# Reading the moving operand of TensorE's products in two interleaved strands

## The chip, the cores and the metric

One Trainium2 chip, one core of it. The metric is device microseconds of one execution of the whole kernel: median of 3 runs 882.95 us (882.77 to 883.12). The profile is that of one execution.

## The reference

```python
# 8 batches, 8 heads, 576 tokens, head size 64
kv  = einsum('bhsd,bhse->bhde', k, v)
out = einsum('bhsd,bhde->bhse', q, kv)
rms = sqrt(mean(out * out, axis=-1, keepdims=True) + 1e-06)
x   = (out / rms * g_norm)            # heads side by side: 4608 tokens x 512
h   = x @ w_in                        # 512 x 2048
P   = a[0] + a[1]*h + a[2]*h*h + a[3]*h*h*h
Q   = 1 + |b[0]|*|h| + |b[1]|*h*h
out = (P / (Q + 1e-06)) @ w_out       # 2048 x 512
```

A linear attention, normalised, and then a feed-forward layer with a rational function between its two large products.

## The kernel before

The 4608 tokens are nine tiles `t` of 512. The 2048 hidden columns are sixteen chunks `c` of 128. A pair (t, c) is a **slot**, and the loop at line 808 walks the 144 slots in order. Everything is issued by hand in the order of the code (line 709), so each engine works through its own queue in that order, and the engines wait for one another by semaphores alone.

In slot i the loop issues, for TensorE, first `gemm2` of the slot two back (L537: chunk c's 128 columns of g times four token blocks, into the four accumulators `acc`), then whatever part of the attention of the next tile stands at this c (tables `attention0` and `attention2`, L439 to L451), and then `gemm1` of the next slot (L468: 128 columns of h for 512 tokens, into `ph`). ScalarE, VectorE and GpSimd work on the slot's own h: `ew_a`, `ew_b`, `ew_c` and `ew_d` (L489 to L532) evaluate the rational function. Their first instruction in a slot is ScalarE's L494, which reads `ph`; their last are L530 (high part of g, ScalarE) and L531 (low part of g, GpSimd), issued a slot later.

**Precision.** From chunk 4 of tile 0 on for `gemm1`, and from chunk 12 of tile 0 on for `gemm2`, each operand is split into a high and a low float32r part, and a product is three TensorE instructions: high times high, low times high, high times low. `gemm1` of a slot is then 4 x 3 = 12 instructions of L486, `gemm2` 4 x 3 = 12 of L551 (L596 at the very end): 24 in a slot, each with its own weight load of 128 columns and 512 moving columns. Before those chunks a product is one plain float32 instruction (L479 and L544), while the split weights are still being made.

**What moves and what stays.** In `gemm1` the stationary operand is a 128 x 128 block of w_in, and the moving one is x (`x[t][kc]`, or `xf` where it is plain): 128 partitions by 512 tokens. In `gemm2` the stationary operand is a 128 x 128 block of g, and the moving one is w_out's chunk: 128 partitions by 512 columns. So far both are read in the order in which they lie.

**The attention** of tile t+1 runs in the slots of tile t. `att_o` (L373) multiplies the kv matrices with q, which lies as 128 partitions by 512 tokens, in two runs of columns where a tile takes tokens of two batches (64 t of the earlier batch, the rest of the later one); from tile 2 on each run is three instructions (L385 to L387), in tile 1 one (L381). Its result, its squares, the sums of squares (L406), the normalised `xf` and its split into x keep the order in which q's tokens lie. At chunk 9 the kv products of a later batch and the sums of squares stand (L344, L406). At chunk 14 ScalarE casts the next tile's x (L249).

**The end of a tile.** At chunk 1 of the next tile, after the last `gemm2` of a tile, `evacuate` (L553) has ScalarE and VectorE copy the four accumulators out (L560, L558); the next `gemm2`, chunk 0 of the new tile, writes the same four banks.

**Tile 0** also converts the weights from 64-bit words and splits them, by the table `first_tiles` (L153).

On the host, `kernel()` (L853) lays q out as `qT` (L868) and w_out in chunks (L878).

Of the kernel before, what the change touches and what calls it, by code (L numbers as in the profile page):

```python
# [23 lines left out]
def linear_attention_then_rational_ffn(  # L24
# [10 lines left out]
    PE, ACT, DVE, POOL = nc.tensor, nc.scalar, nc.vector, nc.gpsimd  # L35

    NB, NPAIR = kv.shape[:2]
    NT, DM = out.shape
    NF = w_in.shape[0]
    P = 128  # L40
    D = 64
    S = NT // NB
    TW = 512
# [28 lines left out]
    kvf = wpool.tile([P, 2, NPAIR, P], F32, tag="f7", name="kvf")  # L72
# [47 lines left out]
    def unsplit1(t, c):  # L120
        return t == 0 and c < 4
# [67 lines left out]
    raws, ups, w32, whl, wparts = {}, {}, {}, {}, {}  # L189
# [129 lines left out]
    xs, x = {}, {}  # L319
    kvq, qs, sqs, rs, rbs, xf = {}, {}, {}, {}, {}, {}  # L320
# [3 lines left out]
    def fetch_kv(t, p):  # L324
        kvms[t, p] = m = work.tile([P, 2, 5, P], F32, tag="kvm", name=f"kvm_{t}_{p}", bufs=NPAIR)
        nc.sync.dma_start(m, kv[t, p])
# [40 lines left out]
    def att_kvp(t, p):  # L367
        if t + 1 < NB:
            kv_products(t + 1, p, kvps[t + 1][:, p])
            if t + 2 < NB:  # L370
                fetch_kv(t + 2, p)

    def att_o(t, p):  # L373
        ps = ps_at.tile([P, TW], F32, tag="at", name=f"op_{t}_{p}", bufs=1)
        q = qs.pop((t, p))
        n0 = D * t
        for bt, cs in ((t - 1, slice(0, n0)), (t, slice(n0, TW))):
            if cs.start == cs.stop:
                continue
            if t == 1:  # L380
                PE.matmul(ps[:, cs], kvf[:, bt, p], q[:, cs], start=True, stop=True)  # L381
                continue
            qh, ql = q
            kh, kl = kvh[bt % 2][:, p], kvl[bt % 2][:, p]
            PE.matmul(ps[:, cs], kh, qh[:, cs], start=True, stop=False)  # L385
            PE.matmul(ps[:, cs], kl, qh[:, cs], start=False, stop=False)  # L386
            PE.matmul(ps[:, cs], kh, ql[:, cs], start=False, stop=True)  # L387
        sq = work.tile([P, TW], F32, tag="at", name=f"sq_{t}_{p}", bufs=4)
        xf[t, p] = xpool.tile([P, TW], F32, tag=f"xf{p}", name=f"xf_{t}_{p}")
        ACT.activation(sq, ps, AF.Square)  # L390
        ACT.activation(xf[t, p], ps, AF.Copy, scale=ghalf)
        sqs[t, p] = sq
        if t == 1:
            next_q(t, p)
# [62 lines left out]
    acc = {}  # L457
# [6 lines left out]
    def in_turn(behind, n):  # L464
        each = [(k, j) for k in range(n) for j in range(3) if j != behind]
        return each if behind is None else each + [(k, behind) for k in range(n)]

    def gemm1(t, c):  # L468
        if t == NTILE - 1 and c % 3 == 2:
            ph = ps_at.tile([P, TW], F32, tag="at", name=f"h_{t}_{c}", bufs=1)  # L470
        else:
            ph = ps_h.tile([P, TW], F32, tag="h", name=f"h_{t}_{c}")
        gemm1_part(t, c, ph, slice(0, TW))
        return ph

    def gemm1_part(t, c, ph, cs, kcs=range(NPAIR)):
        if unsplit1(t, c):
            for kc in kcs:
                PE.matmul(ph, w32["wi", c][:, kc * P:(kc + 1) * P], xf[t, kc], start=(kc == 0), stop=(kc == NPAIR - 1))  # L479
            return  # L480
        order = in_turn(behind1.get((t, c)), NPAIR)
        for n, (kc, j) in enumerate(order):
            xh, xl = (f[:, cs] for f in x[t][kc])
            wh, wl = (f[:, kc * P:(kc + 1) * P] for f in whl["wi", c])
            w, f = ((wh, xh), (wl, xh), (wh, xl))[j]
            PE.matmul(ph, w, f, start=(n == 0), stop=(n == len(order) - 1))  # L486
# [50 lines left out]
    def gemm2(t, c):  # L537
        g = gs.pop((t, c))
        first, last = c == 0, c == NF - 1
        if first:  # L540
            acc[t] = [ps_acc.tile([P, DM], F32, tag="acc", name=f"acc_{t}_{s}") for s in range(NSUB)]
        if unsplit2(t, c):
            for s in range(NSUB):
                PE.matmul(acc[t][s], g[:, s * P:(s + 1) * P], w32["wo", c], start=first, stop=last)  # L544
            return
        (gh, gl), (wh, wl) = g, whl["wo", c]
        products = (gh, wh), (gh, wl), (gl, wh)
        order = in_turn(behind2.get((t, c)), NSUB)
        for n, (s, j) in enumerate(order):
            a, w = products[j]  # L550
            PE.matmul(acc[t][s], a[:, s * P:(s + 1) * P], w, start=first and j == 0, stop=last and all(k != s for k, _ in order[n + 1:]))  # L551

    def evacuate(t):  # L553
        for k in range(NSUB // 2):
# [9 lines left out]
    def finish(t, ph):  # L564
        c = NF - 1
        parts = [slice(k * TW // 2, (k + 1) * TW // 2) for k in range(2)]
        rooms = ("d", 2), ("q", 2), ("u", 2), ("gh", 2), ("gl", 2)
        spare = ("qr", 1), ("qh", 1), ("ql", 1), ("rb", 2), ("rb", 2)
        halves = []
        for n, tags in enumerate((rooms, spare)):  # L570
            new = [work.tile([P, TW // 2], F32 if m < 3 else F32R, tag=tag, name=f"{'vquab'[m]}_last_{n}", bufs=bufs) for m, (tag, bufs) in enumerate(tags)]
            halves.append((*new, ps_at.tile([P, TW // 2], F32, tag=("r", "at")[n], name=f"r_last_{n}", bufs=1)))
        for k, (v, q, u, gh, gl, r) in zip(parts, halves):
            ACT.activation(v, ph[:, k], AF.Abs, scale=b1)
            ACT.activation(u, ph[:, k], AF.Identity, bias=na[:, 2:3], scale=na[:, 3:4])
        ew_d(t, c - 1)
        for k, (v, q, u, gh, gl, r) in zip(parts, halves):
            DVE.scalar_tensor_tensor(q, v, b0abs, ph[:, k], ALU.add, ALU.mult)
            DVE.tensor_tensor(u, u, ph[:, k], ALU.mult)
            DVE.scalar_tensor_tensor(u, u, na[:, 1:2], ph[:, k], ALU.add, ALU.mult)  # L580
            ACT.activation(q, q, AF.Abs)
            ACT.activation(r, q, AF.Ln, bias=bias[:, 2:3], scale=QSC)
            ACT.activation(r, r, AF.Exp, bias=bias[:, 3:4], scale=-1.0)
        gemm2(t, c - 2)
        for v, q, u, gh, gl, r in halves:
            DVE.scalar_tensor_tensor(u, u, na[:, 0:1], r, ALU.add, ALU.mult)
            DVE.scalar_tensor_tensor(r, q, QEPS, r, ALU.add, ALU.mult)
            DVE.scalar_tensor_tensor(u, r, 2.0, u, ALU.subtract, ALU.mult)
            ACT.copy(gh, u)
            DVE.tensor_tensor(gl, u, f32(gh), ALU.subtract)  # L590

        def products(c, gs, order, s0=0):
            wh, wl = whl["wo", c]
            for s, j in order:
                a, w = ((gs[0], wh), (gs[0], wl), (gs[1], wh))[j]
                PE.matmul(acc[t][s], a[:, (s - s0) * P:(s - s0 + 1) * P], w, start=False, stop=c == NF - 1 and j == 2)  # L596

        def store(s, by):
            ob = work.tile([P, DM], F32, tag="at", name=f"ob_{t}_{s}", bufs=4)
            r0 = t * TW + s * P  # L600
            if by is not None:
                copy(by, ob, acc[t][s])
                nc.sync.dma_start(out[r0:r0 + P], ob)
                return
            for e, (by, queue) in enumerate(((DVE, nc.sync), (ACT, ACT))):
                es = slice(e * DM // 2, (e + 1) * DM // 2)
                copy(by, ob[:, es], acc[t][s][:, es])
                queue.dma_start(out[r0:r0 + P, es], ob[:, es])

        before = gs[t, c - 1]  # L610
        products(c - 1, before, [(s, j) for s in range(2) for j in range(3)])
        products(c, halves[0][3:5], [(s, j) for s in range(2) for j in range(2)] + [(s, 2) for s in range(2)])
        store(0, DVE)
        store(1, ACT)
        for s, by in (2, DVE), (3, None):
            products(c - 1, before, [(s, j) for j in range(3)])
            products(c, halves[1][3:5], [(s, j) for j in range(3)], 2)
            store(s, by)
# [140 lines left out]
    conv_b2(("wi", 2), one)  # L759
    scale_low(("wi", 2), ACT, two)  # L760
    h00 = ps_h.tile([P, TW], F32, tag="h", name="h_0_0")
    gemm1_part(0, 0, h00, slice(0, TW), (0,))
    first_rb(1)
    first_warm(3, 1)
    first_rb(3)
# [3 lines left out]
    scale_low(("wo", 0), ACT, both)  # L769
    first_norm(3)  # L770
    scale_high(("wi", 2), DVE, two)
    gemm1_part(0, 0, h00, slice(0, TW), (1,))
    conv_b2(("wi", 0), two)
    first_rb(2)
    first_norm(2)
    gemm1_part(0, 0, h00, slice(0, TW), (2,))
    gemm1_part(0, 0, h00, slice(0, TW), (3,))
    fetch_kv(1, 0)
    fetch_q(1, 0)
    for u in fetch_at[-1]:  # L780
# [4 lines left out]
    ph = h00  # L785
# [22 lines left out]
    for i, (t, c) in enumerate(slots[:-1]):  # L808
# [12 lines left out]
        if i < 4:  # L821
            ph = gemm1(0, i + 1)
        if t + 1 < NTILE:
# [4 lines left out]
            if i == MOVE[0]:  # L828
                last = work.tile([P, 2 * DM], F32, tag="rb", name="w_last", bufs=2)
# [6 lines left out]
        if t == NTILE - 1:  # L836
            ahead += [gemm1(*slots[k]) for k in ((i + 1, i + 2) if c == 0 else (i + 2,)) if k < len(slots)]
            ph = ahead.pop(0) if ahead else None
        elif i >= 4:
            ph = gemm1(*slots[i + 1])  # L840
        if c == NF - 2 and 0 < t < NTILE - 1:
            xl = [split(t + 1, p) for p in range(NPAIR)]
# [48 lines left out]
```

## Time and profile before

| | |
|---|---|
| median of 3 runs | 882.95 us |
| span of the profiled execution | 881.1 us |
| TensorE busy (matmul) | 873.4 us, 99% |
| TensorE weight loads | 694.1 us, 79% |
| VectorE / ScalarE / GpSimd busy | 684.2 / 696.7 / 330.5 us |
| DMA | 65.93 MB, mean 75 GB/s |

The page gives a matmul's duration from its start to its modelled end, which lies in the next one or two; so the busy share of TensorE says little, and the time that a product takes is read as the distance from one start to the next. Engine names: PE is TensorE, PEld its weight load, ACT ScalarE, DVE VectorE, POOL GpSimd.

### The profile page before, as it was taken

Reading aid. Unit: us, or ns where it says so; the run is one execution under the profiler, and the core shown is the slowest. Engines: PE = TensorE matmul, PEld = TensorE weight load, DVE = VectorE, ACT = ScalarE, POOL = GpSimd, SP = SyncE. Lnnn points to the kernel's source line nnn. Section 1 sums busy time; section 2 is a strip of 40 time slices with the busy share of each in tenths; the row PEclk is TensorE's granted clock in tenths of the full one; section 3 lists DMA queues with packets and bytes.
Section 4 is the critical chain, followed back from the end, with each engine's and each line's share of the span. In section 5 each row is a group of like instructions: output and inputs, shape, how many; then the busy total and the mean of one; then the engine's idle time right before and its main releaser. Section 6 shows DMA issues by size and latency. Waiting matters only on the chain.

```text
span 881.1 us, 11990 instructions
## 1 busy us (share of the span) xinstructions
PE 873.4 (99%) x4370; PEld 694.1 (79%) x4370; DVE 684.2 (78%) x1022; ACT 696.7 (79%) x1129; POOL 330.5 (38%) x265
## 2 busy tenths in 40 slices
PE   8999999999999999999999999999999999999998
PEld 5466578888888888888888888888888878788886
DVE  3999998968876788668866886588767877787876
ACT  5999889878886778867886888678877788778775
POOL 3586672525242333224332423242433333332221
PEclk9999999999999999999999999999999999999999
DMA  9683541131111302050103211020102010101001
GB/s 361 261 322 132 146 154 73 36 132 49 48 36 61 120 1 72 25 166 3 60 24 133 49 48 36 14 49 21 52 25 49 1 63 22 49 1 48 1 1 48
DMA packets 24191, 65.93 MB, mean 75 GB/s; under 512 B 2372, under 2 KB 2756, under 8 KB 24132
## 3 DMA queue, kind: packets, MB, share of 16 engines
q1 hardware_dynamic: 23968, 65.04, 21.9%
q8 instruction: 34, 0.56, 0.3%
q14 instruction: 25, 0.20, 0.1%
q10 hardware_dynamic: 164, 0.14, 0.0%
HBM read 55.59 MB, written 9.57 MB: 74 GB/s over the span
## 4 chain that ended last, share of the span: by engine, by line
PE 96%; DVE 2%; ACT 1%; issue 0%; POOL 0%; ACTq 0%; DVEq 0%; POOLq 0%
PE h L486 43%; PE acc L551 39%; PE acc L544 5%; PE ms L344 2%; PE h L479 1%; PE ms L406 1%; PE op L386 1%; PE op L387 1%; PE op L385 1%; PE kvp L653 1%; PE acc L596 1%; PE op L381 0%; PE op L662 0%; PE idle L644 0%; PE rb L701 0%; DVE q L497 0%
## 5 line engine op out<-in xcount | busy, mean ns | idle before, releaser
L486 PE MATMUL h<-x,wiparts 128*128 128x512 f32 x1680 | 409.8, 393 | 0.0
L486 PEld LDWEIGHTS h<-x,wiparts 128*128 128x128 f32 x1680 | 313.4, 188 | 70.4 <-issue 4.6
L531 POOL TENSOR_TENSOR gl<-u,gh 128x512 fp32r<-128x512 f32 x131 | 172.1, 1314 | 431.6 <-ACT gh L530 355.3
L513 DVE SCALAR_TENSOR_TENSOR u<-u,na,r 128x512 f32<-128x512 f32 x143 | 106.6, 745 | 85.5 <-ACT r L507 85.3
L497 DVE SCALAR_TENSOR_TENSOR q<-v,b0abs,h 128x512 f32<-128x512 f32 x143 | 106.2, 743 | 72.3 <-ACT u L495 71.3
L494 ACT ACTIVATE v<-h,b 128x512 f32<-128x512 f32 x143 | 98.6, 690 | 79.0 <-PE h L486 78.6
L551 PE MATMUL acc<-woparts,gh 128*128 128x512 f32 x400 | 124.8, 391 | 0.4 <-ACT ob L560 0.4
L551 PE MATMUL acc<-woh,gh 128*128 128x512 f32 x320 | 124.7, 390 | 0.0
L551 PE MATMUL acc<-woh,gl 128*128 128x512 f32 x320 | 124.6, 390 | 0.0
L503 ACT ACTIVATE q<-q 128x512 f32<-128x512 f32 x143 | 90.5, 633 | 40.7 <-DVE q L497 39.4
L551 PE MATMUL acc<-wol,gh 128*128 128x512 f32 x320 | 122.2, 390 | 0.0
L495 ACT ACTIVATE u<-h,na 128x512 f32<-128x512 f32 x143 | 111.0, 776 | 0.0
L504 DVE SCALAR_TENSOR_TENSOR u<-u,na,h 128x512 f32<-128x512 f32 x143 | 106.9, 748 | 5.1
L530 ACT CAST gh<-u 128x512 fp32r<-128x512 f32 x131 | 81.3, 620 | 34.9 <-DVE u L520 24.7
L506 ACT ACTIVATE r<-q,bias 128x512 f32<-128x512 f32 x143 | 99.0, 692 | 4.5
L514 DVE SCALAR_TENSOR_TENSOR r<-q,r 128x512 f32<-128x512 f32 x143 | 98.4, 688 | 0.0
L507 ACT ACTIVATE r<-r,bias 128x512 f32<-128x512 f32 x143 | 94.7, 662 | 4.7
L498 DVE TENSOR_TENSOR u<-u,h 128x512 f32<-128x512 f32 x143 | 97.3, 680 | 0.0
L520 DVE SCALAR_TENSOR_TENSOR u<-r,u 128x512 f32<-128x512 f32 x131 | 90.5, 691 | 4.2
L551 PEld LDWEIGHTS acc<-woparts,gh 128*128 128x128 f32 x400 | 74.6, 188 | 17.8 <-ACT r L507 1.6
L551 PE MATMUL acc<-woparts,gl 128*128 128x512 f32 x200 | 78.0, 390 | 0.0
L551 PEld LDWEIGHTS acc<-woh,gh 128*128 128x128 f32 x320 | 60.1, 188 | 12.4
(139 smaller groups left out, 869.6 us busy)
## 6 DMA issues: line engine op xcount, KB each, us to landing
kvm<-in_kv_dram SPq DMA_DIRECT2D x28, 640.0 KB
raw_wo<-in_w_out_dram SPq DMA_DIRECT2D x8, 1024.0 KB
qr<-in_qT_dram SPq DMA_DIRECT2D x32, 256.0 KB
rb<-rd SPq DMA_DIRECT2D x32, 256.0 KB
out_dram<-ob SPq DMA_DIRECT2D x16, 512.0 KB
raw_wi<-in_w_in_dram SPq DMA_DIRECT2D x6, 1024.0 KB
first<-in_first_dram SPq DMA_DIRECT2D x4, 640.0 KB
raw_wi<-in_w_in_dram SPq DMA_DIRECT2D x4, 512.0 KB
```

Of the source, the lines that this page charges most:

```text
L486: PE.matmul(ph, w, f, start=(n == 0), stop=(n == len(order) - 1))
L494: ACT.activation(v, ph, AF.Abs, scale=b1)
L495: ACT.activation(u, ph, AF.Identity, bias=na[:, 2:3], scale=na[:, 3:4])
L497: DVE.scalar_tensor_tensor(q, v, b0abs, ph, ALU.add, ALU.mult)
L498: DVE.tensor_tensor(u, u, ph, ALU.mult)
L504: DVE.scalar_tensor_tensor(u, u, na[:, 1:2], ph, ALU.add, ALU.mult)
L506: ACT.activation(r, q, AF.Ln, bias=bias[:, 2:3], scale=QSC)
L507: ACT.activation(r, r, AF.Exp, bias=bias[:, 3:4], scale=-1.0)
L513: DVE.scalar_tensor_tensor(u, u, na[:, 0:1], r, ALU.add, ALU.mult)
L514: DVE.scalar_tensor_tensor(r, q, QEPS, r, ALU.add, ALU.mult)
L531: POOL.tensor_tensor(gl, u, f32(gh), ALU.subtract)
L551: PE.matmul(acc[t][s], a[:, s * P:(s + 1) * P], w, start=first and j == 0, stop=last and all(k != s for k, _ in order[n + 1:]))
```

## The change

Both large stages read their moving operand through `strands`: the 512 columns are taken as two halves, and the order is column 0 of the first half, column 0 of the second, column 1 of the first, and so on. Two consecutive columns lie 256 columns (1024 bytes) apart. So that results come out in their true order, the host lays q's tokens and w_out's columns out in the inverse order: of each 512, the even ones first and then the odd ones. All that comes between q and x keeps that order. `att_o` has a tile's tokens of two batches in two runs in each half, and reads and writes each run as two blocks, one in each half; the number of columns per instruction is the same. The number of instructions, their sizes, the DMA transfers and the work of the other engines stay as they are.

```diff
+    def halves(f):
+        return f.rearrange("p (a b) -> p a b", a=2)
+
     def att_o(t, p):
...
-        n0 = D * t
-        for bt, cs in ((t - 1, slice(0, n0)), (t, slice(n0, TW))):
+        n0 = D * t // 2
+        for bt, cs in ((t - 1, slice(0, n0)), (t, slice(n0, TW // 2))):
             if cs.start == cs.stop:
                 continue
+            to = halves(ps)[:, :, cs]
             if t == 1:
-                PE.matmul(ps[:, cs], kvf[:, bt, p], q[:, cs], start=True, stop=True)
+                PE.matmul(to, kvf[:, bt, p], halves(q)[:, :, cs], start=True, stop=True)
                 continue
-            qh, ql = q
+            qh, ql = (halves(f)[:, :, cs] for f in q)
             kh, kl = kvh[bt % 2][:, p], kvl[bt % 2][:, p]
-            PE.matmul(ps[:, cs], kh, qh[:, cs], start=True, stop=False)
+            PE.matmul(to, kh, qh, start=True, stop=False)
...
+    def strands(f):
+        return f.rearrange("p (a b) -> p b a", a=2)
+
...
-                PE.matmul(ph, w32["wi", c][:, kc * P:(kc + 1) * P], xf[t, kc], start=(kc == 0), stop=(kc == NPAIR - 1))
+                PE.matmul(ph, w32["wi", c][:, kc * P:(kc + 1) * P], strands(xf[t, kc]), start=(kc == 0), stop=(kc == NPAIR - 1))
...
-            xh, xl = (f[:, cs] for f in x[t][kc])
+            xh, xl = (strands(f) for f in x[t][kc])
...
-                PE.matmul(acc[t][s], g[:, s * P:(s + 1) * P], w32["wo", c], start=first, stop=last)
+                PE.matmul(acc[t][s], g[:, s * P:(s + 1) * P], strands(w32["wo", c]), start=first, stop=last)
...
-            PE.matmul(acc[t][s], a[:, s * P:(s + 1) * P], w, start=first and j == 0, stop=last and all(k != s for k, _ in order[n + 1:]))
+            PE.matmul(acc[t][s], a[:, s * P:(s + 1) * P], strands(w), start=first and j == 0, stop=last and all(k != s for k, _ in order[n + 1:]))
...
-    qT = q.reshape(B, H // 2, 2, S, D).transpose(1, 2, 4, 0, 3).reshape(H // 2, 2 * D, B * S)
+    qT = q.reshape(B, H // 2, 2, S, D).transpose(1, 2, 4, 0, 3).reshape(H // 2, 2 * D, B * S // 512, 256, 2)
+    qT = qT.swapaxes(3, 4).reshape(H // 2, 2 * D, B * S)
...
-        "w_out": w_out.view(_np.int64).reshape(DF // 128, 128, DM),
+        "w_out": w_out.view(_np.int64).reshape(DF // 128, 128, DM // 2, 2).swapaxes(2, 3).reshape(DF // 128, 128, DM),
```

The line of the last products (L596) takes `strands(w)` in the same way.

## Rows read from the trace of the kernel before

**Rows 1.** The page: busy shares, and the granted clock in 40 slices.

```profile
PE 873.4 (99%) x4370; PEld 694.1 (79%) x4370; DVE 684.2 (78%) x1022; ACT 696.7 (79%) x1129; POOL 330.5 (38%) x265
...
PEclk9999999999999999999999999999999999999999
```

**Rows 2.** The page: the chain that ended last, by engine and by line.

```profile
PE 96%; DVE 2%; ACT 1%; issue 0%; POOL 0%; ACTq 0%; DVEq 0%; POOLq 0%
```

**Rows 3.** Timeline of PE, tile 3: start us, us, engine, line, operation, count.

```profile
357.40 2.88 PE L486 MATMUL h<-x,wiparts 128*128 128x512 f32 x12
360.12 0.39 PE L551 MATMUL acc<-woh,gh 128*128 128x512 f32 x1
```

**Rows 4.** Timeline of PE, tile 3: the attention's products with 256 moving columns.

```profile
351.33 0.28 PE L386 MATMUL op<-qh,kvl 128*128 128x256 f32 x1
...
351.93 0.63 PE L486 MATMUL h<-x,wiparts 128*128 128x512 f32 x2
```

**Rows 5.** Plain float32 products: timeline of PE in tile 0, and their group's mean.

```profile
71.14 3.59 PE L544 MATMUL acc<-wow,g 128*128 128x512 f32 x8
L544 PE MATMUL acc<-wow,g 128*128 128x512 f32 x96 | 43.3, 594 | 0.0
```

**Rows 6.** Timeline of PE, tile 6: the 12 products right behind an att_o.

```profile
647.04 3.02 PE L486 MATMUL h<-x,wiparts 128*128 128x512 f32 x12
649.89 0.39 PE L551 MATMUL acc<-woh,gh 128*128 128x512 f32 x1
```

**Rows 7.** Busy time by stretch: tile 0, tile 1 to chunk 8, tile 3's chunks 2 to 13.

```profile
26.40:132.50 106.10, 105.57 (x496) 64.44 (x495) 103.17 (x137) 95.44 (x151) 75.29 (x44) 1.00 0.55 195
132.50:184.60 52.10, 52.10 (x239) 43.42 (x238) 47.50 (x72) 46.86 (x78) 20.71 (x16) 1.00 0.15 50
331.30:403.60 72.30, 72.30 (x410) 60.08 (x410) 52.34 (x79) 55.82 (x92) 25.30 (x20) 1.00 0.25 81
```

**Rows 8.** ACT's waits for h: tile 1 to chunk 8, tile 1 from there, tile 3's chunks 2 to 13.

```profile
ACT v L494 <- PE h L486: 0.5, 1, 0.5
ACT v L494 <- PE h L486: 7.8, 5, 5.0
L494 ACT ACTIVATE v<-h,b 128x512 f32<-128x512 f32 x12 | 8.3, 690 | 10.5 <-PE h L486 10.5
```

**Rows 9.** Timeline around a tile's end: ACT at chunk 14 and at the copies out.

```profile
403.62 0.69 ACT L494 ACTIVATE v<-h,b 128x512 f32<-128x512 f32 x1 [1.21 <-PE h L486]
...
410.15 0.68 ACT L494 ACTIVATE v<-h,b 128x512 f32<-128x512 f32 x1
...
415.42 0.68 ACT L494 ACTIVATE v<-h,b 128x512 f32<-128x512 f32 x1
...
420.28 0.68 ACT L494 ACTIVATE v<-h,b 128x512 f32<-128x512 f32 x1
...
425.14 1.07 ACT L560 COPY ob<-acc 128x512 f32<-128x512 f32 x2
```

**Rows 10.** Timeline of PE at the same place in tile 3: the first gemm2 of a tile.

```profile
330.57 0.84 PE L486 MATMUL h<-x,wiparts 128*128 128x512 f32 x3
331.34 0.47 PE L551 MATMUL acc<-woparts,gh 128*128 128x512 f32 x1
```

**Rows 11.** Timeline of ACT in tile 7: three slots with attention in them.

```profile
718.39 0.69 ACT L494 ACTIVATE v<-h,b 128x512 f32<-128x512 f32 x1 [0.30 <-PE h L486]
724.51 0.69 ACT L494 ACTIVATE v<-h,b 128x512 f32<-128x512 f32 x1 [0.30 <-PE h L486]
730.63 0.69 ACT L494 ACTIVATE v<-h,b 128x512 f32<-128x512 f32 x1 [0.30 <-PE h L486]
```

**Rows 12.** Groups of instructions by line: the products of att_o.

```profile
L385 PE MATMUL op<-qh,kvh 128*128 128x128 f32 (+7 forms) x52 | 15.2, 293 | 0.0
L381 PE MATMUL op<-qr,kvf 128*128 128x64 f32 (+1 forms) x16 | 4.6, 408 | 0.0
```

**Rows 13.** Timeline at tile 4's start: a low part of g, and its first reader.

```profile
418.40 1.30 POOL L531 TENSOR_TENSOR gl<-u,gh 128x512 fp32r<-128x512 f32 x1 [4.49 <-ACT gh L530]
...
420.19 0.39 PE L551 MATMUL acc<-woparts,gl 128*128 128x512 f32 x1
```

More of the change, by code (lines that the diff above doesn't have):

```diff
@@ L375, in att_o @@
         q = qs.pop((t, p))
-        n0 = D * t
-        for bt, cs in ((t - 1, slice(0, n0)), (t, slice(n0, TW))):
+        n0 = D * t // 2
+        for bt, cs in ((t - 1, slice(0, n0)), (t, slice(n0, TW // 2))):
             if cs.start == cs.stop:
                 continue
+            to = halves(ps)[:, :, cs]
             if t == 1:
-                PE.matmul(ps[:, cs], kvf[:, bt, p], q[:, cs], start=True, stop=True)
+                PE.matmul(to, kvf[:, bt, p], halves(q)[:, :, cs], start=True, stop=True)
                 continue
-            qh, ql = q
+            qh, ql = (halves(f)[:, :, cs] for f in q)
             kh, kl = kvh[bt % 2][:, p], kvl[bt % 2][:, p]
-            PE.matmul(ps[:, cs], kh, qh[:, cs], start=True, stop=False)
-            PE.matmul(ps[:, cs], kl, qh[:, cs], start=False, stop=False)
-            PE.matmul(ps[:, cs], kh, ql[:, cs], start=False, stop=True)
+            PE.matmul(to, kh, qh, start=True, stop=False)
+            PE.matmul(to, kl, qh, start=False, stop=False)
+            PE.matmul(to, kh, ql, start=False, stop=True)
         sq = work.tile([P, TW], F32, tag="at", name=f"sq_{t}_{p}", bufs=4)
@@ L472, in gemm1, with gemm1_part @@
             ph = ps_h.tile([P, TW], F32, tag="h", name=f"h_{t}_{c}")
-        gemm1_part(t, c, ph, slice(0, TW))
+        gemm1_part(t, c, ph)
         return ph
-    def gemm1_part(t, c, ph, cs, kcs=range(NPAIR)):
+    def gemm1_part(t, c, ph, kcs=range(NPAIR)):
         if unsplit1(t, c):
             for kc in kcs:
-                PE.matmul(ph, w32["wi", c][:, kc * P:(kc + 1) * P], xf[t, kc], start=(kc == 0), stop=(kc == NPAIR - 1))
+                PE.matmul(ph, w32["wi", c][:, kc * P:(kc + 1) * P], strands(xf[t, kc]), start=(kc == 0), stop=(kc == NPAIR - 1))
             return
@@ L595, in products @@
                 a, w = ((gs[0], wh), (gs[0], wl), (gs[1], wh))[j]
-                PE.matmul(acc[t][s], a[:, (s - s0) * P:(s - s0 + 1) * P], w, start=False, stop=c == NF - 1 and j == 2)
+                PE.matmul(acc[t][s], a[:, (s - s0) * P:(s - s0 + 1) * P], strands(w), start=False, stop=c == NF - 1 and j == 2)
         def store(s, by):
@@ L761, in linear_attention_then_rational_ffn @@
     h00 = ps_h.tile([P, TW], F32, tag="h", name="h_0_0")
-    gemm1_part(0, 0, h00, slice(0, TW), (0,))
+    gemm1_part(0, 0, h00, (0,))
     first_rb(1)
@@ L771, in linear_attention_then_rational_ffn @@
     scale_high(("wi", 2), DVE, two)
-    gemm1_part(0, 0, h00, slice(0, TW), (1,))
+    gemm1_part(0, 0, h00, (1,))
     conv_b2(("wi", 0), two)
@@ L775, in linear_attention_then_rational_ffn @@
     first_norm(2)
-    gemm1_part(0, 0, h00, slice(0, TW), (2,))
-    gemm1_part(0, 0, h00, slice(0, TW), (3,))
+    gemm1_part(0, 0, h00, (2,))
+    gemm1_part(0, 0, h00, (3,))
     fetch_kv(1, 0)
```

## The prediction

> **What bounds the kernel now.** I read the busy shares and the clock first. TensorE counts as busy 99% of the span and its granted clock is full, 2.4 GHz, in all 40 slices [rows 1]; the chain that ended last lies 96% on it [rows 2]. A matmul's end is modelled, so neither says that a product takes the time that it must. For that I go to the timeline and take distances between starts. In a steady stretch twelve products begin at 357.40 and the next thing at 360.12 [rows 3]: 2.72 us / 12 = 226.7 ns a product. At 2.4 GHz 512 columns are 213.3 ns, so 13.3 ns, 32 cycles, go into something else, and this happens 3264 times: 140 of the 144 slots have a split gemm1 and 132 a split gemm2, 12 each.
>
> Is this excess per column or per product? The attention's products with half as many columns answer it: five starts from 351.33 to 351.93 [rows 4] are 120 ns each, and 256 columns are 106.7, so again 13.3. It is per product, and each product has one weight load of 128 columns beside it. The plain float32 products show something else: eight take 3.59 us [rows 5], less the last one's 0.594 that is 3.00 / 7 = 428 ns from start to start, 2 x 214: two passes, with an excess of about 1 ns each, though a weight load runs beside them too. So the excess belongs to products that consume one fresh 4-byte column per cycle, and goes where each column is held for two. A third reading: right behind an att_o, with the weight loads at another phase to the products, the same twelve take 2.85 us [rows 6], 237.5 ns each. Twelve products of one kind with the same neighbours differ by 5% with that phase alone. My reading is that weight loads and the moving operand get in each other's way at the memory, about 32 cycles a product when steady.
>
> **Where a shorter product would show.** By stretch [rows 7]: in tile 0 VectorE is busy 103.17 of 106.10 us, so the conversions set the pace and TensorE's time there is worth nothing. In tile 1 up to chunk 8 ScalarE waits for h only once, 0.5 us [rows 8]: the elementwise chain is level with TensorE, and a faster product gains nothing. From there on ScalarE waits for h in nearly every slot: 7.8 us in the rest of tile 1, 10.5 us in the twelve slots of tile 3 from chunk 2 to 13 [rows 8]. Those are bound by TensorE. Around the end of each tile it is the other way: from chunk 14's h, for which ScalarE waited 1.21 us, the next three slots start with no wait at all, and the chain runs on to the copies of the accumulators at 425.14, 21.5 us later [rows 9]. The new tile's first gemm2 waits for these copies already now: its first start comes where three steady products would end it, 330.57 + 3 x 0.227 = 331.25, and is seen at 331.34, and it lasts 0.47 us in place of 0.39 [rows 10]: 0.17 us in all. TensorE's four slots there can get faster and will only wait longer.
>
> **The change part by part.** *Removed and added:* no instruction. *The moving order* is the one term that counts. No row shows a product that reads two strands, so I bound it. Best case by the nearest row: the excess goes as in the plain float32 products, 428 / 2 = 214 ns, a gain of 12.7 ns (226.7 - 214). Worst case by the nearest row: 237.5 ns, a loss of 10.8, if the weight loads collide as in the stretch behind att_o. Far worst: every column costs as much as in a plain float32 product, 428 ns, a loss of 201. I take the best case. Two strands 1024 bytes apart mean that each place in memory is visited every second cycle, which is what the float32 products do by holding each column for two, and those lose nothing to the same loads.
>
> [...]
>
> *Sum.* Tiles 2 to 8: twelve slots of 24 products, from the first gemm2 behind the copies to the h that starts the next boundary (in tile 8, to the last h, behind which the closing elementwise chain is fixed): 288 x 12.7 ns = 3.66 us, times 7 = 25.6 us. Tile 1: the five slots in which ScalarE waits, 120 x 12.7 ns = 1.5 us. Tile 0, the start, tile 1 to chunk 8 and the boundaries: nothing. Total 27.1 us, for 2136 products.
>
> *Is there cover for it?* A slot gets 24 x 12.7 = 305 ns shorter. ScalarE's tightest waits are 0.30 us in tile 7's attention slots [rows 11]: just enough, to within their rounding. At the boundary four slots of TensorE shrink by 1.2 us in all, which becomes a wait for the copies. Before that, a low part of g is finished at 419.70 and first read at 420.19 [rows 13], 0.49 us to spare, less than the 0.9 us by which TensorE comes earlier there; this stall only takes part of the later one's place.
>
> *att_o's blocks:* 156 instructions of L385 to L387 (three lines of 52) and 16 of L381 [rows 12] read and write two blocks in place of one. At zero, as the columns are as many; above, if each block cost like a product of its own with its 13.3 ns, 172 x 13.3 = 2.3 us, exposed; below zero nothing, since no weight load is saved. *Plain float32 products* (L479, L544) are 128 and lie in tile 0 and ahead of it; they take two cycles a column already, so zero, and at most a doubling to 856 ns, 55 us, part of it beside VectorE. *Host layout:* same bytes and run lengths in every transfer, zero.
>
> The profile's span is 881.1 us; the median of the runs, 882.95, is 1.85 above it, which I leave as it is. 882.95 - 27.1 = 855.9, so **856 us**, 3.1% less.
>
> **The rivals.** *No change.* If the 32 cycles are the array's own turn from one set of weights to the next, at the rate of one column a cycle, the order of the columns is indifferent, and the time is 883. For it: the excess is the same at 256 and 512 columns. Against: the 237.5 ns behind att_o, which a fixed cost would not give. [...]
>
> *Slower.* [...] It decides as soon as a product takes over 227 ns, because TensorE has no slack in tiles 1 to 8: 3072 products there. At 237.5 ns that is 3072 x 10.8 = +33 us, 916 us; at 428 ns 3072 x 201 = +617 us, about 1500 us, plus what tile 0 can't hide. For it: in this kernel's rows every operand of a product is read in order, so nothing shows that another order is free. [...]
>
> **How the numbers follow.** The gain 0.60, no change 0.15, slower 0.25 (half of it around 916, half far above). The forecast's own range is 848 to 870: down to 848 if boundaries and tile 1 shrink too (3072 x 12.7 = 39 us is the ceiling, 844), up to 870 if half of the 13.3 ns goes. The range over the cases is 848 to 918: it takes in no change and the near end of slower, and leaves out the far end and a little of the gain's tails, about 0.18. A difference under 0.2% can't be told from none by a measurement of this kernel; faster by more than that 0.60, within 0.15, slower 0.25.
>
> **What would show it.** Right: twelve products of L486 in a steady slot from start to start take about 2.57 us in place of 2.72; ScalarE's waits for h in chunks 2 to 13 fall from 10.5 us a tile to 7; TensorE's gap at the first gemm2 of a tile grows from 0.17 to over 1 us; tile 0 keeps its 106 us. Wrong: the 2.72 us stay (no change), or rise (slower); if they fall and tile times don't, an elementwise chain that I took to have room has none.

## The result and the profile after

The changed kernel takes **867.94 us** (867.73 to 868.07, 4 runs) against 882.89 us of the kernel before on the same chip: a ratio of 0.9829, with an interval of 0.9815 to 0.9843. It is 15 us faster, where 27 were forecast. The span of the profiled execution goes from 881.1 to 866.3 us. Two effects of opposite sign make up this difference of 14.8 us, and both can be read from the trace.

The page of the changed kernel, busy shares and the chain that ended last (against [rows 1, 2]):

```profile
PE 853.2 (98%) x4370; PEld 696.0 (80%) x4370; DVE 687.7 (79%) x1022; ACT 699.3 (81%) x1129; POOL 328.1 (38%) x265
...
PE 61%; DVE 19%; ACT 17%; issue 2%; DMA 1%; SPq 0%; ACTq 0%; DVEq 0%
```

The chain lay 96% on TensorE and now lies 61% on it: the elementwise engines end more of the waits. Line numbers have moved: L486 is now L493, L551 is L558, L479 and L544 are L486 and L551, L494 is L501.

The timeline of TensorE in the changed kernel (start us, us, engine, line, operation, count): plain products in tile 0, the first gemm2 of tile 3, a steady gemm1 with the attention's products ahead of it, and a gemm1 behind an att_o in tile 6:

```profile
36.21 4.58 PE L551 MATMUL acc<-wow,g 128*128 128x512 f32 x8
...
330.71 0.48 PE L558 MATMUL acc<-woparts,gl 128*128 128x512 f32 x1 [0.33 <-POOL gl L538]
...
332.97 2.75 PE L493 MATMUL h<-x,wiparts 128*128 128x512 f32 x12
336.22 0.67 PE L558 MATMUL acc<-woparts,gh 128*128 128x512 f32 x2 [0.50 <-ACT r L514]
...
355.26 0.28 PE L390 MATMUL op<-qh,kvl 128*128 128x256 f32 x1
...
355.85 2.75 PE L493 MATMUL h<-x,wiparts 128*128 128x512 f32 x12
358.44 0.38 PE L558 MATMUL acc<-woh,gh 128*128 128x512 f32 x1
...
641.00 2.84 PE L493 MATMUL h<-x,wiparts 128*128 128x512 f32 x12
643.68 0.38 PE L558 MATMUL acc<-woh,gh 128*128 128x512 f32 x1
```

Read the distances. Twelve split products take from 355.85 to 358.44: 2.59 us, **215.8 ns each**, where they took 226.7 [rows 3]. Behind an att_o they take 2.68 us where they took 2.85 [rows 6]. There the first of the twelve stands apart, as the shortest, middle and longest modelled lengths show (ns; the kernel before, then the changed one). Each such length is 163 ns more than the distance to the next start, to within 2 ns:

```profile
L486 PE MATMUL h<-x,wiparts x12: 387/395/477, 647.0 to 649.7; 128*128 128x512 f32 x12
L493 PE MATMUL h<-x,wiparts x12: 379/379/462, 641.0 to 643.5; 128*128 128x512 f32 x12
```

The first product takes 314 ns in order and 299 in strands. The other eleven take 224 to 236 ns in order, but 215 or 216 throughout in strands.

The plain float32 products went the other way. The first eight of tile 0, in the kernel before, and the whole group's mean in the changed one:

```profile
34.62 3.70 PE L544 MATMUL acc<-wow,g 128*128 128x512 f32 x8
...
L551 PE MATMUL acc<-wow,g 128*128 128x512 f32 x96 | 54.0, 705 | 0.0
```

The same eight take 4.58 us instead of 3.70, and the mean length is 705 ns instead of 594 [rows 5]. From start to start, the first of the eight left out, it is **540 ns instead of 428**. The attention's products of 256 columns, which now read and write two blocks, still follow one another at 118 ns (355.26 to 355.85, five starts; 120 in [rows 4]).

Busy time by stretch in the changed kernel (length; then PE, PEld, DVE, ACT and POOL busy; clock, DMA share, GB/s): tile 0, tile 1 to chunk 8, the boundary of tiles 2 and 3, tile 3's chunks 2 to 13. The last line is ScalarE's wait for the h of a split gemm1 in tile 0 (us in all, times, longest):

```profile
27.00:142.40 115.40, 115.40 (x493) 64.26 (x492) 107.92 (x137) 97.94 (x149) 75.00 (x44) 1.00 0.49 176
142.40:193.80 51.40, 51.26 (x245) 44.63 (x244) 46.84 (x72) 46.48 (x76) 20.52 (x16) 1.00 0.16 54
329.00:337.00 8.00, 7.17 (x33) 5.67 (x32) 7.16 (x12) 6.93 (x12) 2.57 (x2) 1.00 0.00 0
336.20:405.20 69.00, 68.98 (x409) 60.38 (x410) 51.32 (x78) 55.91 (x91) 24.10 (x19) 1.00 0.26 85
...
ACT v L501 <- PE h L493: 6.5, 5, 2.3
```

Tile 1's first chunk starts at 142.4 us instead of 132.5: **9.9 us lost up to there**. From there to the end the kernel needs 723.9 us instead of 748.6: **24.7 us won**. Tile 3's twelve slots shrink from 72.3 to 69.0 us [rows 7]. In tile 0 of the kernel before, no wait of ScalarE for h is longer than 0.1 us.

ScalarE in the changed kernel: its group L501 in tile 3's chunks 2 to 13 (busy, mean ns, idle before and who ended it), and its timeline over the end of tile 3:

```profile
L501 ACT ACTIVATE v<-h,b 128x512 f32<-128x512 f32 x12 | 8.3, 688 | 6.8 <-PE h L493 6.5
```

```profile
405.22 0.69 ACT L501 ACTIVATE v<-h,b 128x512 f32<-128x512 f32 x1 [0.38 <-PE h L493]
...
426.97 1.07 ACT L567 COPY ob<-acc 128x512 f32<-128x512 f32 x2
```

The wait for h fell from 10.5 us [rows 8] to 6.5. From chunk 14's h to the copies it is 21.75 us, as it was (21.5 in [rows 9]): this stretch belongs to the elementwise chain. TensorE now waits there, 0.33 us for a low part of g at 330.71, and then again at 336.22: the block that began at 332.97 needs 2.59 us, up to 335.56, so 0.66 us pass before the first gemm2 of the new tile.

### The profile page after: what moved, and what is told of

Same layout as the page of the kernel before. It is cut to its first block, busy times and chain, and to the rows that moved or that the text cites. A ratio compares the mean times of both kernels' runs of the same rounds, so it can differ in the third digit from the quotient of the medians.

```text
span 866.3 us, 11993 instructions
## 1 busy us (share of the span) xinstructions
PE 853.2 (98%) x4370; PEld 696.0 (80%) x4370; DVE 687.7 (79%) x1022; ACT 699.3 (81%) x1129; POOL 328.1 (38%) x265
## 4 chain that ended last, share of the span: by engine, by line
PE 61%; DVE 19%; ACT 17%; issue 2%; DMA 1%; SPq 0%; ACTq 0%; DVEq 0%
PE h L493 24%; PE acc L558 21%; PE acc L551 6%; ACT r L513 5%; ACT r L514 4%; DVE u L520 4%; ACT q L510 4%; DVE q L504 4%; DVE r L521 4%; DVE u L527 4%; PE h L486 2%; DVE x L316 2%; PE ms L344 2%; PE ms L410 1%; PE op L391 1%
## 5 line engine op out<-in xcount | busy, mean ns | idle before, releaser
L493 PE MATMUL h<-x,wiparts 128*128 128x512 f32 x1680 | 390.2, 382 | 0.0
L493 PEld LDWEIGHTS h<-x,wiparts 128*128 128x128 f32 x1680 | 315.2, 189 | 50.4 <-issue 4.1
L501 ACT ACTIVATE v<-h,b 128x512 f32<-128x512 f32 x143 | 98.3, 688 | 55.8 <-PE h L493 53.4
L558 PE MATMUL acc<-woparts,gh 128*128 128x512 f32 x400 | 120.3, 380 | 3.5 <-ACT r L514 2.5
L558 PE MATMUL acc<-woh,gh 128*128 128x512 f32 x320 | 121.3, 379 | 0.0
L558 PE MATMUL acc<-woh,gl 128*128 128x512 f32 x320 | 121.3, 379 | 0.0
L558 PE MATMUL acc<-wol,gh 128*128 128x512 f32 x320 | 118.9, 379 | 0.4 <-POOL wol L269 0.4
L558 PEld LDWEIGHTS acc<-woparts,gh 128*128 128x128 f32 x400 | 75.1, 189 | 16.2 <-ACT r L514 4.3
L558 PE MATMUL acc<-woparts,gl 128*128 128x512 f32 x200 | 76.9, 384 | 1.7 <-POOL gl L538 1.5
L558 PEld LDWEIGHTS acc<-wol,gh 128*128 128x128 f32 x320 | 60.5, 189 | 9.3 <-POOL wol L269 0.8
```

The source lines that it names most:

```text
L558: PE.matmul(acc[t][s], a[:, s * P:(s + 1) * P], strands(w), start=first and j == 0, stop=last and all(k != s for k, _ in order[n + 1:]))
```

## The experiments

Eleven kernels were run. Two questions stood behind them: is the loss of 9.9 us in tile 0 the plain products' own, and why does a split product gain 10.9 ns?

### The two kinds of products apart

`a_split_only`: strands for the split products; the plain ones, and with them all w_out products of tile 0, in order. Tile 0's order is put right where g is written and where its accumulators are copied out.

```diff
-                PE.matmul(ph, w32["wi", c][:, kc * P:(kc + 1) * P], strands(xf[t, kc]), ...)
+                PE.matmul(ph, w32["wi", c][:, kc * P:(kc + 1) * P], xf[t, kc], ...)
...
-                PE.matmul(acc[t][s], g[:, s * P:(s + 1) * P], strands(w32["wo", c]), ...)
+                PE.matmul(acc[t][s], g[:, s * P:(s + 1) * P], w32["wo", c], ...)
...
-            PE.matmul(acc[t][s], a[:, s * P:(s + 1) * P], strands(w), ...)
+            PE.matmul(acc[t][s], a[:, s * P:(s + 1) * P], strands(w) if t else w, ...)
...
+        if unsplit1(t, c):
+            g, r, u = g.rearrange("p (b a) -> p a b", a=2), halves(r), halves(u)
         DVE.scalar_tensor_tensor(g, r, 2.0, u, ALU.subtract, ALU.mult)
...
+                if t == 0:
+                    ACT.copy(ob[:, s].rearrange("p (b a) -> p a b", a=2), halves(acc[t][2 * k + s]))
```

> Strands for the split products only; the plain float32 products of tile 0, and all of tile 0's w_out products, read in order again (the order is put right where g of chunks 0 to 3 is written and where tile 0's accumulators are copied out). Theory one, the plain products pay for the strands: they go from 540 ns back to 428 ns from start to start, 128 x 112 ns = 14 us of TensorE, tile 1 begins near 132.5 us in place of 142.4, and the time is about 858 us. Theory two, tile 0 is late for another reason (the blocks of att_o, or another phase of its waits): tile 1 still begins later than 138 us and the time stays over 864.

Measured: **861.30 us** (861.06 to 861.49, 5 runs), 0.9756 of the kernel before (0.9743 to 0.9769), so faster than both kernels. Its tile 0 by stretch, and two groups by line (busy us, mean ns, idle before; the second one of tile 0 alone, and under it the same group in the kernel before):

```profile
26.30:135.30 109.00, 104.84 (x496) 64.23 (x495) 106.00 (x137) 97.77 (x150) 75.32 (x44) 1.00 0.53 192
```

```profile
L553 PE MATMUL acc<-wow,g 128*128 128x512 f32 x96 | 43.5, 595 | 0.7 <-POOL wow L242 0.7
...
L237 DVE SCALAR_TENSOR_TENSOR wiw<-raw_wi,wiw 128x1024 int32<-128x1024 int32 x6 | 9.8, 1635 | 0.0
...
L237 DVE SCALAR_TENSOR_TENSOR wiw<-raw_wi,wiw 128x1024 int32<-128x1024 int32 x6 | 8.6, 1432 | 0.0
```

The plain products are back (mean 595 ns as in [rows 5], 705 in the changed kernel), and tile 1 starts at 135.3: 7.1 of the 9.9 us return, and the time is 3.3 us over the 858 of theory one. From there to the end it takes 724.2 us, against 723.9 in the changed kernel: the 24.7 us won are kept. Theory two asked for over 138 and over 864, and falls. What is left, 2.8 us, lies where VectorE sets the pace: the same 137 instructions are busy 106.00 us instead of 103.17 [rows 7]. The six of L237 for w_in, for one, take 1635 ns each where they took 1432. All its conversions in tile 0 (L211, L232, L237, L242, L269) take 43.4 us instead of 40.2. They are longer in the changed kernel and in `b_plain_only` too (45.4 and 43.4 us), which don't put tile 0's order right, so that edit doesn't explain it. Why the conversions got longer stays open.

`b_plain_only` is the opposite: strands in the plain products alone.

```diff
-            xh, xl = (strands(f) for f in x[t][kc])
+            xh, xl = x[t][kc]
...
-            PE.matmul(acc[t][s], a[:, s * P:(s + 1) * P], strands(w), ...)
+            PE.matmul(acc[t][s], a[:, s * P:(s + 1) * P], w, ...)
```

> Strands for the plain float32 products of tile 0 only; all split products read in order (tokens and columns come out in mixed order). Theory one, the plain products' loss is their own: 540 ns, tile 1 begins near 142 us, split products 226.7 ns, and the time is about 893 us, 10 over the kernel before. Theory two, tile 0's loss comes from elsewhere: tile 1 begins near 133 us and the time is about 883.

Measured: 895.28 us in one run. Tile 0 of it by stretch, ScalarE's wait for h there, and TensorE's timeline:

```profile
27.00:144.80 117.80, 117.80 (x493) 64.03 (x492) 107.21 (x138) 95.91 (x149) 73.72 (x44) 1.00 0.48 172
...
ACT v L501 <- PE h L493: 11.9, 8, 2.6
```

```profile
36.19 4.58 PE L551 MATMUL acc<-wow,g 128*128 128x512 f32 x8
...
358.45 2.91 PE L493 MATMUL h<-x,wiparts 128*128 128x512 f32 x12
361.20 0.39 PE L558 MATMUL acc<-woh,gh 128*128 128x512 f32 x1
```

The plain products have the 4.58 us of the changed kernel, and tile 1 starts at 144.8, 12.3 us late. Theory one holds, from both sides. ScalarE's wait shows how: it waits 11.9 us for h in tile 0, where it had no such wait in the kernel before, so TensorE has become the slower one there. Of the 2.4 us over the changed kernel's 142.4, some 1.7 go with tile 0's 156 split products of gemm1, which are in order here (an estimate: 156 x 10.9 ns). From tile 1 to the end it takes 748.7 us, as the kernel before does (748.6). It has the host's layout and att_o's blocks of the changed kernel, so neither of these costs anything that shows.

### Which order helps

Five kernels read all products in other orders. Only the line in `strands` changes:

```diff
-        return f.rearrange("p (a b) -> p b a", a=2)
+        return f.rearrange("p (c a b) -> p c b a", a=2, b=4)   # p_near
+        return f.rearrange("p (a b) -> p b a", a=4)            # p_quarters
+        return f.rearrange("p (b a) -> p a b", a=2)            # p_evenodd
+        return f.rearrange("p (a b k) -> p b a k", a=2, k=2)   # p_pairs
+        return f.rearrange("p (a b k) -> p b a k", a=2, k=4)   # p_lines
```

What was expected:

> All products read in strands that lie only 16 bytes apart: columns 0, 4, 1, 5, 2, 6, 3, 7 and so on (tokens and columns come out in another order). Theory one, any order in which columns that follow one another are no neighbours: 216 ns for split products. Theory two, the places must be far apart: 227 ns or more. Plain products: 540 ns if leaving the neighbour is what costs them.

> All products read four strands of 128 columns, 512 bytes apart, in place of two of 256 (tokens and columns come out in another order). Theory one, any order in which two columns that follow one another are no neighbours in memory frees the split products: 216 ns again. Theory two, the two places must be exactly two, or 1024 bytes apart: over 220 ns, up to 227 or more. Plain products: if they pay for every column that leaves its neighbour, 540 ns again; if they pay per strand, more.

> All products read the even columns and then the odd ones, a step of 8 bytes (tokens and columns come out in another order). Theory one, any order in which columns that follow one another are no neighbours: 216 ns for split products. [...] Plain products: 428 ns if one walk suffices, 540 if leaving the neighbour is what costs.

> All products read two strands 1024 bytes apart, but two neighbouring columns of each at a time (tokens and columns come out in another order). Theory one, changing the place at each column is what frees the split products: between 216 and 227 ns. Theory two, two places in alternation are enough at any grain: 216 ns. Plain products: half of the loss, about 484 ns, if each change of place costs; 540 if the second place costs.

> All products read two strands 1024 bytes apart, four neighbouring columns of each at a time (tokens and columns come out in another order). Theory one, changing the place at each column is what frees the split products: 227 ns, as in order. Theory two, two places in alternation are enough at any grain: 216 ns. Plain products: about 456 ns if each change of place costs the same, 428 if a group of four columns is as good as a walk in order.

Measured, in this order: 868.12, 1107.79, 1617.57, 1230.37 and 956.20 us, one run each. Timelines of TensorE, one fence for each kernel in the same order: eight plain products, then a split gemm1 and what follows it.

```profile
36.19 4.61 PE L551 MATMUL acc<-wow,g 128*128 128x512 f32 x8
...
397.44 2.75 PE L493 MATMUL h<-x,wiparts 128*128 128x512 f32 x12
400.03 0.38 PE L558 MATMUL acc<-woh,gh 128*128 128x512 f32 x1
```

```profile
44.01 7.23 PE L551 MATMUL acc<-wow,g 128*128 128x512 f32 x8
...
400.53 3.45 PE L493 MATMUL h<-x,wiparts 128*128 128x512 f32 x12
403.81 0.44 PE L558 MATMUL acc<-woh,gh 128*128 128x512 f32 x1
```

```profile
34.93 3.87 PE L551 MATMUL acc<-wow,g 128*128 128x512 f32 x8
...
404.30 5.65 PE L493 MATMUL h<-x,wiparts 128*128 128x512 f32 x12
409.77 0.64 PE L558 MATMUL acc<-woh,gh 128*128 128x512 f32 x1
```

```profile
34.89 3.89 PE L551 MATMUL acc<-wow,g 128*128 128x512 f32 x8
...
402.66 4.17 PE L493 MATMUL h<-x,wiparts 128*128 128x512 f32 x12
406.66 0.83 PE L558 MATMUL acc<-woparts,gh 128*128 128x512 f32 x2
```

```profile
34.38 3.70 PE L551 MATMUL acc<-wow,g 128*128 128x512 f32 x8
...
395.78 3.17 PE L493 MATMUL h<-x,wiparts 128*128 128x512 f32 x12
398.79 0.41 PE L558 MATMUL acc<-woh,gh 128*128 128x512 f32 x1
```

The distance from the first start of a gemm1 to what follows, by twelve, beside the median distance between the starts of two plain products of gemm2 in that kernel's trace. The eight plain products shown include a longer first one each; in the kernel before, the first such eight take 3.70 us.

| order of the 512 columns | split, ns each | plain, ns each |
|---|---|---|
| as they lie | 226.7 | 429 |
| two strands, 1024 bytes apart | 215.8 | 540 |
| two strands, 16 bytes apart | 215.8 | 543 |
| two strands, four columns of each at a time | 251 | 429 |
| two strands, two columns of each at a time | 333 | 453 |
| four strands, 512 bytes apart | 273 | 873 |
| even columns, then odd ones | 456 | 451 |

The medians over all split products of gemm1 agree with the second column to within about 1%, except for four strands, where the median is 283 ns.

No theory of the pair covers this. "Any order in which neighbours don't follow one another" is refuted by the even columns, 456 ns, and by four strands, 273 ns. "The two places must lie far apart" is refuted by the strands 16 bytes apart, which do as well as those 1024 apart, 215.8 ns both. And two places in alternation are not enough either: with two or four columns at a time they lose, at 333 and 251 ns against 226.7. Of the orders tried, what helps is narrow: two strands, one column at a time.

The plain products rank the orders otherwise. As they lie, or with four columns of each strand at a time, one takes 429 ns. With two at a time, or in even columns, it takes 451 to 453. By single columns it takes 540 and 543 in two strands, 26% more, and 873 in four. Why is not shown by any run.

### What the excess in order belongs to

`w_half` loads half as many stationary columns for a third of the gemm1 products of the kernel before, from tile 1 on, and leaves the other half of these products out; `w_half_strands` does the same to the changed one.

```diff
-            PE.matmul(ph, w, f, start=(n == 0), stop=(n == len(order) - 1))
+            half = slice(0, P // 2 if t and j == 1 else P)
+            PE.matmul(ph[half], w[:, half], f, start=(n == 0), stop=(n == len(order) - 1))
```

> The kernel before, all operands read in order, but from tile 1 on the products of w_in's low part load and use only 64 of their 128 stationary columns (half of those products is left out of h). Their weights load beside the product in front of them. Theory one, the excess is collisions between the weight load and the moving operand, one cycle for every four stationary columns: the product beside which the half load runs takes 213.3 + 6.7 = 220 ns from start to start in place of 226.7. Theory two, the excess is a fixed turn between two products: 226.7 ns as before.

> The changed kernel, with the products of w_in's low part from tile 1 on loading and using only 64 of their 128 stationary columns (half of those products is left out of h). In order the same edit made products uneven, 224 to 236 ns by their place among the twelve. Theory one, strands make a product independent of when its neighbour's weights are loaded: 216 ns at every place, a gemm1 of 2.59 us. Theory two, strands only suit the one even rhythm of loads: uneven again, over 2.65 us.

Measured: 887.16 us with the operand in order, 4.3 over its kernel before, and 868.23 us with strands (one run each; 883.09 for the kernel before beside the second). Timelines of TensorE, in order and in strands:

```profile
302.10 2.92 PE L487 MATMUL h<-x,wiparts 128*128 128x512 f32 x12
304.86 0.39 PE L552 MATMUL acc<-woh,gh 128*128 128x512 f32 x1
```

```profile
301.05 2.75 PE L494 MATMUL h<-x,wiparts 128*128 128x512 f32 x12
303.64 0.38 PE L559 MATMUL acc<-woh,gh 128*128 128x512 f32 x1
```

In order both theories miss. Less to load made gemm1 longer: 2.76 us, 230 ns a product, and by its place among the twelve a product took 224 to 236 ns. So the excess isn't a toll of so many cycles for so many loaded columns, and it isn't a fixed turn that nothing can move. In strands the same edit leaves 2.59 us, 215.8 ns at every place. So in these runs the time of a product in order went with the weight loads beside it (224 to 236 ns with half loads, 226.7 without); in strands it didn't (215.8 ns both times). Whether it went with their size or with their moment isn't separated: a half load is shorter (134 ns instead of 188) and also brings only 64 of the 128 stationary columns.

`n384_order` and `n384_strands` cut each gemm1 from tile 1 on into 12 products of 384 columns and 12 of 128, in the kernel before and in the changed one:

```diff
-        for n, (kc, j) in enumerate(order):
+        parts = (slice(0, 384), slice(384, TW)) if t else (slice(0, TW),)
+        for cs, n, kc, j in ((cs, n, *o) for cs in parts for n, o in enumerate(order)):
...
-            PE.matmul(ph, w, f, ...)
+            PE.matmul(ph[:, cs], w, f, ...)
```

> The kernel before, all in order, but from tile 1 on every gemm1 is 12 products of 384 columns and then 12 of 128 instead of 12 of 512. Theory one, the excess of a product in order is fixed, 13.3 ns: 160.0 + 13.3 = 173.3 ns from start to start with 384 columns. Theory two, it goes with the columns, 32 cycles for 512: 160.0 + 10.0 = 170.0 ns. The products of 128 columns take what a weight load takes, 110 to 113 ns.

> The changed kernel with the same cut of every gemm1 from tile 1 on, 384 and 128 columns, each in two strands. 512 columns in strands take 216 ns, 2.4 over the columns' own 213.3. Theory one (strands remove the whole excess and leave about 2.4 ns a product): 162.4 ns with 384 columns. Theory two (what is left goes with the columns): 161.8 ns. Both say that the gain over the same products in order, 173.3 or 170.0, is 8 to 11 ns; a gain of 0 would mean that strands help only at 512 columns.

Timelines of TensorE, a run of products of 384 columns in each, in order and then in strands, and under each the mean length of one (the last ns):

```profile
347.67 2.27 PE L487 MATMUL h<-x,wiparts 128*128 128x384 f32 x12
...
L487 PE MATMUL h<-x,wiparts 128*128 128x384 f32 x1536 | 291.5, 337 | 0.6 <-DVE x L316 0.6
```

```profile
348.11 1.95 PE L494 MATMUL h<-x,wiparts 128*128 128x384 f32 x11
...
L494 PE MATMUL h<-x,wiparts 128*128 128x384 f32 x1536 | 273.9, 327 | 0.0
```

With a single product's 0.337 and 0.327 us taken off, that is 1.93 / 11 = 176 ns in order and 1.62 / 10 = 162 ns in strands; over all 1408 such pairs of each trace the medians are 174 and 163. The excess in order is the fixed one (173.3 expected, 170.0 by the rival), and strands take about 11 ns off a product of 384 columns as off one of 512. The products of 128 columns take about 108 ns in order and 107 in strands: the next gemm2 starts 3.39 and 3.24 us after the first product of 384 columns, and twelve times 174 and 163 ns of that go to these. In the kernel before, weight loads of an att_o follow one another at 110 ns (646.79, 646.90 and 647.01 us, L386, L387 and L486). The times, 977.31 and 949.16 us, are longer because 1536 instructions were added.

## Why the prediction was right, and where a term was not

**The path was right.** TensorE's distance from start to start was the term that counted, and the time came off where it was forecast: 24.7 us from tile 1 on, against 27.1 in the sum. Tile 3's twelve slots lost 3.3 us (3.66 forecast). At the boundaries the elementwise chain stayed, and TensorE's wait grew to 0.33 and 0.66 us from 0.17 (forecast: over 1 us in all). ScalarE's wait for h fell to 6.5 us (forecast 7).

Tile 8 went from 92.5 to 88.8 us, as forecast, but ScalarE had waited only 2.2 us for h there. The larger wait is one that the prediction didn't read (kernel before, from 800.2 us on; us in all, times, longest):

```profile
ACT gh L530 <- PE acc L551: 7.4, 7, 1.1
...
ACT v L494 <- PE h L486: 2.2, 6, 0.4
```

The first is the wait of the cast that writes g's high part, and a gemm2 ended it. Both waits are gone in the changed kernel: ScalarE's chain needs 4.86 us a slot (827.32 to 832.18 us, two starts of L501), and TensorE's further speed is worth nothing there.

That 867.94 us lies within the forecast's own range, 848 to 870, is in part luck. The upper end stood for half of the excess going. But four fifths of it went (10.9 of 13.3 ns), and 9.9 us were lost where the sum had nothing.

**The gain of a product was sized too high.** The step took the excess of the plain float32 products, 1 ns a pass, as what would be left, so 12.7 ns; 10.9 came off. The 2.4 GHz behind the 213.3 ns of 512 columns is in no row, but distances show the same rate: 226.7 ns at 512 columns [rows 3] less 120 at 256 [rows 4] is 106.7 ns for 256, so 0.417 ns a column, 2.4 columns in a ns, which makes 213.3 ns of 512 and leaves 13.3 of excess, and the 384 columns of `n384_order` lie on that line to within 1 ns (174 against 173.3). The 24.7 us measured are 2136 x 10.9 = 23.3 and 1.4 more, half of it in tile 1 up to chunk 8 (52.1 to 51.4 us), where nothing was forecast.

**The step that failed is the one on the plain products**: "they take two cycles a column already, so zero". They take 112 ns more each, 128 x 112 = 14.3 us of TensorE. The bound given with it, a doubling, held. With it fell the sentence that "TensorE's time there is worth nothing". VectorE did set the pace (103.17 of 106.10 us), but TensorE was close behind it, and the longer products made ScalarE wait 6.5 us for h in tile 0, 11.9 in `b_plain_only`, where it hadn't waited. 9.9 of the 14.3 us came out at the end; `a_split_only` gets 7.1 of them back.

**The reason for the gain was half right.** That the excess is per product and not per column is shown (174 and 163 ns at 384 columns). That a product in order takes another time when the weight loads beside it change, and one in strands doesn't, is shown by the two kernels with half loads (224 to 236 against 215.8 ns) and by the products behind an att_o (224 to 236 against 215 or 216, the first left out). The size of that effect was misread: the "237.5 ns each" of the worst case holds a first product of 314 ns, and the other eleven take 231 on the mean. That the excess is collisions in step with the size of the load, as the first theory for `w_half` had it, is refuted: 220 ns were expected and the mean was 230. Whether loads and operand collide at the memory at all isn't shown.

That "each place in memory is visited every second cycle" frees the product was only argued, and the orders by two and four columns, which also alternate between two places (333 and 251 ns), make it doubtful. Its pattern, the plain products, was read in two ways, as "two passes" and as "holding each column for two" cycles; 428 ns fit both, and no run tells them apart. What the memory does stays open.

**The rivals.** *No change* fell with the 215.8 ns. *Slower* came true for the other kind of product, where two strands cost 26% (540 ns against 428), and for the split products in four of the five other orders (251 to 456 ns against 226.7).

## What to carry to other kernels

Read start to start, and for more than one size: 227 ns at 512 columns and 120 at 256 said that the excess was per product, which no busy share says. Look at single distances too: a mean over twelve took one late product for a trait of all. Where one edit touches two kinds of an instruction (split and plain products here), give each a bound and try each alone: they answered with opposite signs, and keeping only the one that gains was worth another 6.6 us (867.94 to 861.30). An engine that is busy 97% of a stretch doesn't make the others free there; how near the next one is decides.

## What the runs showed of the hardware that I had not expected

- A float32r product of 128 x 512 columns, the moving operand read in two strands by single columns, takes 215.8 ns from start to start; as it lies 226.7. The distance of the strands, 16 or 1024 bytes, made no difference.
- Other orders cost far more: 251 to 456 ns, and the whole kernel up to 1617.57 us.
- A plain float32 product of the same size takes 428 ns as it lies and 540 in the same two strands; in even and odd columns, which double the float32r product's time (456 ns), it takes only 451.
- In order, loading half as many weights for every third product of gemm1 made these twelve longer, not shorter (230 instead of 227 ns on the mean); in strands they stayed at 215.8.
- The granted clock stayed at 1.00 through the waits of 0.33 and 0.66 us at the tiles' boundaries.
